# One more pause in the conversion of a MoE1 weight slot: two steps become three

## The chip, the cores and the metric

The kernel runs on one core of a Trainium2 chip. The core has a matrix engine (TensorE, PE in the profile), a vector engine (VectorE, DVE), an activation engine (ScalarE, ACT), a general engine (GpSimd, POOL) and a queue that issues most transfers (SyncE, SP). Each engine works through its own list of instructions in order; engines wait for each other through semaphores. The metric is the device time of one execution in microseconds (us); lower is better.

## The reference

```python
def reference(**kwargs):
    ...
    attn_out = _attn_ref(**attn_kwargs)          # q, k, v: 2 x 12 heads x 448 x 64, causal
    B, H, S, D = attn_out.shape
    x = np.ascontiguousarray(attn_out.transpose(0, 2, 1, 3)).reshape(B * S, H * D)   # 896 x 768
    x = _moe_ref(x=x, **moe_kwargs)              # h = x @ w_in (768 x 2048); h * sigmoid(1.702 h) @ w_out
    return _moe2_ref(x=x, **moe2_kwargs)         # 8 experts, one for each token: relu(x @ w1[e]) @ w2[e]
```

The two weights of the middle part, `w_in` (768 x 2048) and `w_out` (2048 x 768), reach the kernel as 64-bit floats.

## The kernel before

The program is written out by hand, engine by engine, in one order (`tc.manual_schedule()`): what stands earlier in the code stands earlier in each engine's list. It has four stages.

**Attention.** 12 pairs of heads, 7 query blocks a pair: 84 steps `s`, whose place in a pair is `s % 7`. A step puts scores on PE (`qk`, L374), their row maximum on DVE (`nmax`, L386), the exponential on ACT (`P`, L388), the normalisation on DVE (`rc`, L395 and L396) and POOL (`P`, L397), and four steps later the transposition of P on PE (`p_tr`, L405) and its copy out of PSUM (`pT`, L408 on DVE or L410 on ACT). Once a pair `av` (L423) sums the output, which ACT and DVE split into a high and a low part (`xhi`, L429, and `xlo`, L430).

**MoE1, first layer ("l1").** 16 blocks `f` of 128 columns of `w_in`, in four quarters `fq`, each of 6 parts `kk` of the inner dimension. For one `kk` PE does 6 matmuls (L444: high by high, high by low, low by high, each for two groups of tokens). Even blocks take their two PSUM tiles from a ring of three ("sc"), odd blocks from one of four ("tp"): the second tile of an even block is the first tile of the even block before it. After the matmuls of a block, ACT (`g`, L547) and DVE (`g`, L548) empty its PSUM in four pieces.

**MoE1, second layer ("l2").** First part B (256 columns) for 7 groups of tokens `t`, then part A (512 columns) for the same 7; 16 parts `kk` each, three matmuls a part (L587). Every four parts ACT and DVE split one more piece of the hidden layer (`gs`, L516 and L519), three pieces ahead. Small PE transpositions and logits (L627, L639) hang on ACT's copies (`y`, L609, and `yT`, L629).

**MoE2.** The experts' weights come as 32-bit floats into 24 places and are split by ACT and DVE (`split`, L307 and L308). The first of them are called for in part A as soon as the last slot of MoE1 is converted (`fill`).

**The weight slots of MoE1.** 48 pieces of `w_in` and `w_out` (24 for l1, 8 for part B, 16 for part A), 128 x 512, are converted from 64-bit floats into a high and a low part: DVE puts the bits together in `w` (L226, L228, L232), ACT rounds `w` into the high part (L234), DVE subtracts it for the low part (L235). One such conversion is a Python generator (`work`, in `add64`). `Stream.pump(n)` adds n to a credit and draws the generator on by one step for each whole credit, at places written into the other stages: at `s % 7` = 3 and 6 in attention, once for each `kk` in l1 (twice in the last quarter), and at the small rates `R2` and `R3` in l2. A step that starts a slot needs a free place in a ring of 19 (`RA`); if there is none, the step does nothing. When the generator ends, the slot is ready, its raw buffer (5, `RAW`) is given back and the next load is put on SP's list (`prefetch`). The subtraction is kept in `st.late` and put on DVE's list in the first step of the slot that follows. A slot that is needed and not ready is drawn to its end at once (`need`).

Of the kernel before, what the change touches and what calls it, by code (L numbers as in the profile page):

```python
# [115 lines left out]
def kernel(ctx, tc, q, k, v, w_in, w_out, w_gate, w_og, w1, w2, out):  # L116
# [49 lines left out]
    with tc.manual_schedule():  # L166
# [43 lines left out]
        def raw_tile(where, shape, dt):  # L210
            if where == "raw":
                return raws.tile(shape, dt, name="raw", tag="raw", bufs=RAW)
            return ringA.tile(shape, dt, name="rawA", tag=f"slotA{where}")

        def add64(keys, src, two=False, ring="A"):
            def load(where):
                raw = raw_tile(where, [128, 512], I64)
                nc.sync.dma_start(raw.rearrange("p (a n) -> p a n", a=2) if two else raw, src)
                return raw

            def work(keys, raw):
                slot = st.slots[keys[0]] = ring_slot(keys[0])
                r = raw.bitcast(U32).rearrange("p (n two) -> p n two", two=2)
                w = raws.tile([128, 512], F32, name="w32", tag="w32", bufs=2)
                wu = w.bitcast(U32)
                nc.vector.tensor_scalar(wu, r[:, :, 1], 3, 0x3FFFFFF8,  # L226
                                        op0=ALU.logical_shift_left, op1=ALU.bitwise_and)
                nc.vector.scalar_tensor_tensor(wu, r[:, :, 1], 0xC0000000, wu,  # L228
                                               op0=ALU.bitwise_and, op1=ALU.bitwise_or)
                st.flush()  # L230
                yield
                nc.vector.scalar_tensor_tensor(wu, r[:, :, 0], 29, wu,  # L232
                                               op0=ALU.logical_shift_right, op1=ALU.bitwise_or)
                nc.scalar.copy(slot[:, 0], w)  # L234
                st.late = keys[0], lambda: nc.vector.tensor_sub(slot[:, 1], w, slot[:, 0].bitcast(F32))  # L235

            st.add(keys, ring, load, work)
# [3 lines left out]
        def ring_slot(key):  # L241
            ring, place = st.home[key]
            if ring == "A":
                return ringA.tile([128, 2, 512], F32R, name="slotA", tag=f"slotA{place}")
            return xr_p[0].tile([128, 2, 512], F32R, name="slotX", tag=f"slotX{place}")
# [792 lines left out]
```

## Time and profile before

| | |
|---|---|
| median of 3 runs | 625.28 us (625.07 to 625.89) |
| the profiled execution's own time | 625.63 us |
| its span, first to last instruction | 623.5 us |
| PE busy | 590.3 us (95%) |
| DVE busy | 463.9 us (74%) |
| ACT busy | 376.9 us (60%) |
| mean granted TensorE clock | 0.987 |

The busy time of PE is modelled at the ends of its matmuls, so a busy PE can still be held up a little. Idle time of an engine counts only where the engine that sets the end waits too. A row of the timeline shows when an instruction started and how long it took, and in brackets how long its engine had been idle and whose result ended that.

### The profile page before, as it was taken

Reading aid. Unit: us, or ns where it says so; the run is one execution under the profiler, and the core shown is the slowest. Engines: PE = TensorE matmul, PEld = TensorE weight load, DVE = VectorE, ACT = ScalarE, POOL = GpSimd, SP = SyncE. Lnnn points to the kernel's source line nnn. Section 1 sums busy time; section 2 is a strip of 40 time slices with the busy share of each in tenths; the row PEclk is TensorE's granted clock in tenths of the full one; section 3 lists DMA queues with packets and bytes.
Section 4 is the critical chain, followed back from the end, with each engine's and each line's share of the span. In section 5 each row is a group of like instructions: output and inputs, shape, how many; then the busy total and the mean of one; then the engine's idle time right before and its main releaser. Section 6 shows DMA issues by size and latency. Waiting matters only on the chain. (4 is left out here: it accounts for less than half of the span.)

```text
span 623.5 us, 10060 instructions
## 1 busy us (share of the span) xinstructions
PE 590.3 (95%) x3326; PEld 473.6 (76%) x3326; DVE 463.9 (74%) x942; ACT 376.9 (60%) x743; POOL 106.7 (17%) x225
## 2 busy tenths in 40 slices
PE   7999999899979999889999999989999999999995
PEld 4665665578868888879877777767888888888884
DVE  2788888757858483797633447789998898889886
ACT  4878878623232323455433234678888888888885
POOL 3333333310000000000001002231631111001110
PEclk8999999999979999999999999999999999999998
DMA  5856554216434241433571503359999999999940
GB/s 134 245 125 141 123 126 116 56 57 184 142 111 115 89 136 37 143 116 119 176 263 38 150 17 119 111 183 347 349 368 353 318 383 377 380 381 378 383 161 20
DMA packets 93146, 118.02 MB, mean 189 GB/s; under 512 B 40208, under 2 KB 53408, under 8 KB 93090
## 3 DMA queue, kind: packets, MB, share of 16 engines
q1 hardware_dynamic: 88562, 109.05, 54.7%
q0 software_dynamic: 2512, 5.54, 2.5%
q10 hardware_dynamic: 2016, 2.75, 1.2%
q8 instruction: 28, 0.46, 0.4%
q14 instruction: 28, 0.23, 0.1%
HBM read 114.10 MB, written 7.54 MB: 195 GB/s over the span
## 5 line engine op out<-in xcount | busy, mean ns | idle before, releaser
L587 PE MATMUL py<-slotA,gs 128*128 128x256 f32 (+1 forms) x609 | 112.5, 337 | 1.0 <-DVE gs L519 1.0
L444 PE MATMUL ph<-xhi,slotA 128*128 128x512 f32 (+1 forms) x384 | 97.7, 374 | 5.6 <-DVE g L548 5.6
L587 PEld LDWEIGHTS py<-slotA,gs 128*128 128x128 f32 x609 | 90.8, 190 | 13.6 <-issue 2.6
L444 PEld LDWEIGHTS ph<-xhi,slotA 128*128 128x128 f32 x384 | 70.8, 191 | 16.5 <-issue 6.1
L234 ACT CAST slotA<-w 128x512 fp32r<-128x512 f32 x45 | 27.9, 621 | 63.1 <-DVE w L232 61.4
L308 DVE TENSOR_TENSOR ent<-wraw,ent 128x1024 fp32r<-128x1024 f32 x48 | 57.9, 1221 | 5.8 <-ACT ent L307 5.8
L444 PE MATMUL ph<-xlo,slotA 128*128 128x512 f32 x192 | 56.1, 373 | 0.0
L374 PE MATMUL sc<-kT,qz 128*128 128x64 f32 (+6 forms) x168 | 53.2, 401 | 2.8 <-ACT kT L365 2.4
L388 ACT ACTIVATE P<-sc,nmax 128x64 f32<-128x64 f32 (+6 forms) x84 | 40.3, 479 | 24.5 <-DVE nmax L386 14.7
L548 DVE TENSOR_TENSOR g<-ph,g 128x256 f32<-128x256 f32 x64 | 23.6, 389 | 41.5 <-ACT g L547 41.5
L897 PE MATMUL ps_h<-ent,xh 128*128 128x512 f32 x192 | 54.0, 402 | 0.0
L307 ACT CAST ent<-wraw 128x1024 fp32r<-128x1024 f32 x48 | 49.9, 1053 | 0.0
L519 DVE TENSOR_TENSOR gs<-g,gs 128x512 fp32r<-128x512 f32 x56 | 37.5, 683 | 16.6 <-ACT gs L516 16.6
L397 POOL TENSOR_SCALAR P<-P,rc 128x64 f32<-128x64 f32 (+2 forms) x72 | 36.0, 500 | 69.6 <-DVE rc L396 43.5
L516 ACT CAST gs<-g 128x512 fp32r<-128x512 f32 x56 | 33.8, 618 | 16.3 <-PE py L587 10.6
L386 DVE TENSOR_REDUCE nmax<-sc 128x1 f32<-128x64 f32 (+6 forms) x84 | 34.4, 411 | 10.7 <-PE sc L375 10.7
L547 ACT ACTIVATE g<-ph 128x256 f32<-128x256 f32 x64 | 20.9, 355 | 33.5 <-PE ph L444 17.2
L897 PEld LDWEIGHTS ps_h<-ent,xh 128*128 128x128 f32 x192 | 35.0, 188 | 7.6 <-DVE ent L308 0.3
L308 DVE TENSOR_TENSOR ent<-wrb,ent 128x1024 fp32r<-128x1024 f32 x30 | 36.3, 1223 | 4.7 <-ACT ent L307 4.2
L444 PEld LDWEIGHTS ph<-xlo,slotA 128*128 128x128 f32 x192 | 35.8, 192 | 4.6
L405 PE MATMUL ps_pT<-ident,P 128*128 128x128 f32 x192 | 37.8, 289 | 1.1
L228 DVE SCALAR_TENSOR_TENSOR w<-raw,w 128x512 uint32<-128x512 uint32 x46 | 35.0, 762 | 1.6
(189 smaller groups left out, 1175.5 us busy)
## 6 DMA issues: line engine op xcount, KB each, us to landing
wraw<-in_moe_w_dram SPq DMA_DIRECT2D x66, 512.0 KB
wrb<-in_moe_w_dram SPq DMA_DIRECT2D x48, 512.0 KB
wr<-in_moe_w_dram SPq DMA_DIRECT2D x30, 512.0 KB
raw<-in_moe_w_in_dram SPq DMA_DIRECT2D x24, 512.0 KB
raw<-in_moe_w_out_dram SPq DMA_DIRECT2D x22, 512.0 KB
qraw<-in_q_dram SPq DMA_DIRECT2D x24, 112.0 KB
kraw<-in_k_dram SPq DMA_DIRECT2D x24, 112.0 KB
vraw<-in_v_dram SPq DMA_DIRECT2D x24, 96.0 KB
```

Source lines behind the costliest of these rows:

```text
L228: nc.vector.scalar_tensor_tensor(wu, r[:, :, 1], 0xC0000000, wu, op0=ALU.bitwise_and, op1=ALU.bitwise_or)
L307: nc.scalar.copy(hi, raw)
L308: nc.vector.tensor_sub(lo, raw, hi.bitcast(F32))
L374: nc.tensor.matmul(sc[:, :n], qT[:, j].rearrange("d h p -> d (h p)"), kT[:, :n], start=True, stop=False)
L386: nc.vector.tensor_reduce(nm, sc[:, :n], axis=AX.X, op=ALU.max, negate=True)
L388: nc.scalar.activation(Pb[j][:, :n], sc[:, :n], AF.Exp, bias=nm, scale=1.0, accum_out=sm)
L397: eng[NORM_ENG[j]].tensor_scalar(Pb[j][:, :n], Pb[j][:, :n], rc, 1.0, op0=ALU.mult, op1=ALU.mult)
L405: nc.tensor.transpose(ps[:, c].rearrange("p h q -> p (h q)"), Pb[j][:, c * KC:(c + 1) * KC], ident)
L444: nc.tensor.matmul(p[:, 0:128 * nt], wt, xt[:, kk, 128 * t0:128 * (t0 + nt)], start=kk == 0 and n == 0, stop=kk == KD - 1 and n == 2)
L519: glate.append(lambda: nc.vector.tensor_sub(gs[:, 1], src, gs[:, 0].bitcast(F32)))
L587: nc.tensor.matmul(py[:, :n], gt[:, kk % 4], wt, start=kk == 0 and m == 0, stop=kk == KF - 1 and m == 2)
L897: nc.tensor.matmul(hps[hf], xh[:, k0 + n], wt[:, n], start=k0 + n == 0 and m == 0, stop=False)
```

## The change

A `yield` is put between ACT's rounding and the last statement of the generator.

```diff
                 nc.vector.scalar_tensor_tensor(wu, r[:, :, 0], 29, wu,
                                                op0=ALU.logical_shift_right, op1=ALU.bitwise_or)
                 nc.scalar.copy(slot[:, 0], w)
+                yield
                 st.late = keys[0], lambda: nc.vector.tensor_sub(slot[:, 1], w, slot[:, 0].bitcast(F32))
```

The number of pumps is not changed. The step that is added puts no instruction on DVE, ACT or PE; it ends the generator, which gives back the raw buffer and puts the next load on SP's list. So three draws convert a slot where two did. The order of instructions on PE and on POOL stays as it is. On DVE, ACT and SP the instructions of the slots move to later places among the others; none is added or taken away. Line numbers behind L234 grow by one in the changed kernel (L235 becomes L236, L386 becomes L387, L548 becomes L549).

By the pumps, 12 slots were begun in attention before (11 of them converted to the rounding there), and 8 are now. In l1 before, blocks 1 to 4 converted three slots each, block 5 one, block 6 none, blocks 7 and 8 three each, blocks 9 and 10 none, blocks 11 and 12 three each; now blocks 1 to 11 convert two each, block 12 four and block 13 three. At the end of l1 37 slots are ready in both. In part B 2.4 slots a group at the rate 0.3 become 1.6; the last two slots, of which only the end of the last stood in part A before, are now converted in the first four parts of part A, and `fill` is called four parts later there.

The places on DVE's list follow. In attention, the second pair that is pumped, around the place `s % 7` = 6: `xlo` of the pair before, the maximum of the largest block but one, and behind it the step of a slot. Before:

```order
L430 TENSOR_TENSOR xlo<-ps_o,xhi 128x448
L396 RECIPROCAL rc<-rc 128x1
L386 TENSOR_REDUCE nmax<-sc 128x1
L232 SCALAR_TENSOR_TENSOR w_533<-raw,w_533 128x512
L386 TENSOR_REDUCE nmax<-sc 128x1
```

The same place in the changed kernel:

```order
L431 TENSOR_TENSOR xlo<-ps_o,xhi 128x448
L397 RECIPROCAL rc<-rc 128x1
L387 TENSOR_REDUCE nmax<-sc 128x1
L226 TENSOR_SCALAR w_593<-raw 128x512
L228 SCALAR_TENSOR_TENSOR w_593<-raw,w_593 128x512
L236 TENSOR_TENSOR slotA<-w_382,slotA 128x512
L387 TENSOR_REDUCE nmax<-sc 128x1
```

The three instructions that begin a slot, which stood at `s % 7` = 3 in every pair, stand here in every third pair; that pair has none at `s % 7` = 3.

In l1, DVE's list of block 1 from the first slot up to where the block is emptied. Before, three slots:

```order
L226 TENSOR_SCALAR w_2038<-raw 128x512
L228 SCALAR_TENSOR_TENSOR w_2038<-raw,w_2038 128x512
L235 TENSOR_TENSOR slotA<-w_1979,slotA 128x512
L232 SCALAR_TENSOR_TENSOR w_2038<-raw,w_2038 128x512
L226 TENSOR_SCALAR w_2059<-raw 128x512
L228 SCALAR_TENSOR_TENSOR w_2059<-raw,w_2059 128x512
L235 TENSOR_TENSOR slotA<-w_2038,slotA 128x512
L232 SCALAR_TENSOR_TENSOR w_2059<-raw,w_2059 128x512
L226 TENSOR_SCALAR w_2080<-raw 128x512
L228 SCALAR_TENSOR_TENSOR w_2080<-raw,w_2080 128x512
L235 TENSOR_TENSOR slotA<-w_2059,slotA 128x512
L232 SCALAR_TENSOR_TENSOR w_2080<-raw,w_2080 128x512
```

In the changed kernel, two, and then the four instructions that empty block 1:

```order
L226 TENSOR_SCALAR w_2002<-raw 128x512
L228 SCALAR_TENSOR_TENSOR w_2002<-raw,w_2002 128x512
L236 TENSOR_TENSOR slotA<-w_1900,slotA 128x512
L232 SCALAR_TENSOR_TENSOR w_2002<-raw,w_2002 128x512
L226 TENSOR_SCALAR w_2029<-raw 128x512
L228 SCALAR_TENSOR_TENSOR w_2029<-raw,w_2029 128x512
L236 TENSOR_TENSOR slotA<-w_2002,slotA 128x512
L232 SCALAR_TENSOR_TENSOR w_2029<-raw,w_2029 128x512
L549 TENSOR_TENSOR g_1973<-ph_1993,g_1973 128x2x128
L549 TENSOR_TENSOR g_1974<-ph_1993,g_1974 128x2x128
L549 TENSOR_TENSOR g_1975<-ph_1994,g_1975 128x2x128
L549 TENSOR_TENSOR g_1976<-ph_1994,g_1976 128x128
```

A slot's four instructions stand one after the other in both; four of them have left the block.

## Rows read from the trace of the kernel before

**Rows 1.** Busy time by stage: stretch, its length, each engine, granted clock, DMA share.

```profile
121.00:252.00 131.00, 124.67 (x600) 107.94 (x599) 84.48 (x174) 39.41 (x95) 4.83 (x46) 0.97 0.38 110
252.00:310.00 58.00, 53.35 (x410) 48.87 (x409) 47.83 (x89) 30.42 (x61) 0.74 (x1) 1.00 0.41 129
```

**Rows 2.** The same for a full attention pair, then the first pumped pair.

```profile
39.34:48.81 9.47, 8.96 (x64) 5.67 (x62) 8.23 (x28) 7.59 (x25) 3.42 (x8) 1.00 0.56 129
...
21.06:29.87 8.81, 8.72 (x63) 5.67 (x62) 7.09 (x26) 7.33 (x24) 3.19 (x7) 1.00 0.74 251
```

**Rows 3.** Timeline of DVE, attention: start, duration, what, idle before it.

```profile
40.80 0.41 DVE L226 TENSOR_SCALAR w<-raw 128x512 uint32<-128x512 uint32 x1
41.24 1.01 DVE L228 SCALAR_TENSOR_TENSOR w<-raw,w 128x512 uint32<-128x512 uint32 x1
...
42.77 0.28 DVE L386 TENSOR_REDUCE nmax<-sc 128x1 f32<-128x128 f32 x1
...
45.46 0.54 DVE L386 TENSOR_REDUCE nmax<-sc 128x1 f32<-128x384 f32 x1
45.91 0.76 DVE L232 SCALAR_TENSOR_TENSOR w<-raw,w 128x512 uint32<-128x512 uint32 x1
46.59 0.21 DVE L386 TENSOR_REDUCE nmax<-sc 128x1 f32<-128x64 f32 x1
```

**Rows 4.** Timeline of POOL and PE in the same pair.

```profile
41.05 0.66 POOL L397 TENSOR_SCALAR P<-P,rc 128x448 f32<-128x448 f32 x1 [0.53 <-DVE rc L396]
...
47.31 0.59 POOL L397 TENSOR_SCALAR P<-P,rc 128x384 f32<-128x384 f32 x1 [1.18 <-ACT slotA L234]
...
47.96 0.55 PE L405 MATMUL ps_pT<-ident,P 128*128 128x128 f32 x3
...
49.80 0.97 PE L423 MATMUL ps_o<-pT,vraw 128*64 128x448 f32 x4 [0.41 <-DVE pT L408]
```

**Rows 5.** Timeline of DVE in l1.

```profile
136.30 0.42 DVE L226 TENSOR_SCALAR w<-raw 128x512 uint32<-128x512 uint32 x1
...
166.46 0.42 DVE L226 TENSOR_SCALAR w<-raw 128x512 uint32<-128x512 uint32 x1
...
168.73 0.42 DVE L226 TENSOR_SCALAR w<-raw 128x512 uint32<-128x512 uint32 x1
...
174.32 0.42 DVE L548 TENSOR_TENSOR g<-ph,g 128x256 f32<-128x256 f32 x1 [0.97 <-ACT g L547]
...
176.50 0.42 DVE L226 TENSOR_SCALAR w<-raw 128x512 uint32<-128x512 uint32 x1
```

**Rows 6.** Timeline of PE in l1.

```profile
155.63 0.41 PE L444 MATMUL ph<-xhi,slotA 128*128 128x384 f32 x1 [0.61 <-DVE g L548]
...
168.69 0.99 PE L444 MATMUL ph<-xhi,slotA 128*128 128x512 f32 x4
...
169.93 0.81 PE L444 MATMUL ph<-xhi,slotA 128*128 128x512 f32 x3
175.76 0.66 PE L444 MATMUL ph<-xhi,slotA 128*128 128x384 f32 x1 [5.02 <-DVE g L548]
...
251.81 0.34 PE L444 MATMUL ph<-xhi,slotA 128*128 128x384 f32 x1
```

**Rows 7.** Short stretches in l1, columns as in Rows 1.

```profile
174.00:174.50 0.50, 0.00 (x0) 0.00 (x0) 0.18 (x1) 0.28 (x1) 0.00 (x0) 0.89 0.56 184
...
181.00:181.50 0.50, 0.50 (x3) 0.40 (x3) 0.44 (x2) 0.02 (x1) 0.00 (x0) 0.78 1.06 414
```

**Rows 8.** Timeline of PE in part B of l2.

```profile
257.67 3.62 PE L587 MATMUL py<-slotA,gs 128*128 128x256 f32 x28 [0.97 <-DVE gs L519]
...
277.68 0.44 PE L627 MATMUL ps_yT<-ident,y 128*128 128x128 f32 x2 [1.81 <-ACT y L609]
...
287.69 3.86 PE L587 MATMUL py<-slotA,gs 128*128 128x256 f32 x30
...
294.19 3.86 PE L587 MATMUL py<-slotA,gs 128*128 128x256 f32 x30
```

## Prediction

> **What bounds the kernel now.** I read the page first: PE is busy for 95% of the span, so only the remaining waits can be won or lost by an edit that adds no work. Busy time by stage puts a good part of them where slots are converted: PE is not busy for 6.3 us of l1 (131.0 less 124.67) and for 4.65 us of part B [rows 1]. In attention a pair takes 9.47 us, of which DVE is busy for 8.23, while the first pair that is pumped, which carries no subtraction yet, took 8.81 [rows 2]. So DVE, not PE, sets the pace wherever slots crowd on it. The timelines say how.
>
> In attention, the instructions at the head of a slot take from 40.80 to 42.77, 1.97 us, and the third instruction of the slot takes 0.68 (45.91 to 46.59) [rows 3]. All maxima queue behind them; the chain goes on over ACT, DVE and POOL, and PE waits at its end: the 128x384 normalisation on POOL starts at 47.31, ends at 47.90, and the transposition that needs it starts at 47.96; then PE waits 0.41 for DVE's copy of that transposition [rows 4].
>
> In l1 a slot takes 2.27 us of DVE (166.46 to 168.73), three of them 7.86 up to the first piece of the emptying (174.32), and from there to the next block's first slot 2.18 (176.50) [rows 5]. That is 10.04 for a block. PE needs 1.24 for a `kk` (168.69 to 169.93), 7.44 for a block [rows 6]. With three slots a block, DVE falls 2.6 us back each time until PE has no PSUM to write to: 0.61 at 155.63 and 5.02 at 175.76 [rows 6]. During the second wait the granted clock fell from full (2.4 GHz) to half: it averages 0.89 over 174.0 to 174.5, so it fell near 174.39, and 0.78 over 181.0 to 181.5, so it was back near 181.2 [rows 7]. PE had last worked at 170.74 (169.93 plus 0.81), 3.65 us ahead of the fall. From 175.76 to 181.2 it did half of what it could: 2.7 us lost on top of the wait.
>
> **What the change does.** It adds no instruction; it spreads the same ones. There are four terms.
>
> **Attention, about 2.2 us gained.** The pumps now run through a cycle of three pairs. The first pair is as before (9.47). The second has its 1.97 at the later place and nothing at the earlier one. The third has only the 0.68. The third pair loses DVE's 1.97 and has nothing at the later place; leaving the pair's own waits aside, PE's list of a pair comes to about 8.4: the 8.81 of the first pumped pair [rows 2] less some 0.4 that PE's starts show as gaps in it, which is an estimate. So it gains about 1.0. The second pair is the disputed one. Where 0.68 stood, the head of a slot and a subtraction now stand ahead of the small block's maximum (46.59) [rows 3]. They take 1.66 to 1.97: 2.27 less the 0.61 that its last instruction takes in l1 by the gap between neighbours (an estimate), or as in rows 3. I take 1.75, 1.07 more. The maximum of the 128x384 block, at 45.46, can come some 0.36 sooner, because nothing stood at the earlier place; so 0.7 later remains. That goes straight into POOL's start at 47.31 and PE's at 47.96 [rows 4]. Of this PE would have waited 0.41 a moment later anyway, and DVE's later copy is only about 0.3 late, since ACT has no rounding to do ahead of the small block's exponential. I take 0.2 lost a pair. Ten pairs follow the first: three as before, four of the second kind, three of the third: 3.0 less 0.8. Bounds: if the second kind is as good as the first pumped pair (8.81), four times 0.65 more is gained, 5.6 in all; if it pays all of 1.07 plus 0.1 for an unlucky overlap, 1.7 is lost.
>
> GpSimd may make the later place dearer or cheaper. DVE's second instruction took 1.01 at 41.24 [rows 3] while POOL's 41.05 to 41.71 ran [rows 4]; the whole slot in l1, with POOL idle, takes 2.27, against 1.97 plus 0.68 here. The Trainium skill, "GPSIMD Engine Reference", Specifications, says that GpSimd shares its SBUF interfaces with VectorE and that they contend when a VectorE instruction has two SBUF inputs, as this one has. By the rows alone the head costs 1.75; by that rule, with POOL's work beside it each time, 1.97, and the attention term would be 1.4 instead of 2.2. The trace agrees with the rule in that one overlap and does not show the later place.
>
> **l1, about 1.0 us gained.** Two slots a block make DVE's block 10.04 less 2.27, 7.77 us, against PE's 7.44: 0.33 a block behind instead of 2.6. That is what PSUM run-ahead can hold up to block 11. Then come four slots and three slots, because the last quarter pumps twice for each `kk`. DVE's clock: block 1's first slot at 136.30; its emptying starts 5.59 later (7.86 less 2.27), 141.89; block 11's ten times 7.77 later, 219.59; block 12's first slot at 221.77, its emptying four slots later (10.13) at 231.90. PE resumed 1.44 after such a start (174.32 to 175.76), so block 14's second tile is free at 233.34. PE would want it eight blocks after 170.74, less the 0.6 to 0.8 of the wait at 155.63 that no longer occurs: 229.5. It waits about 3.9 us: one wait for block 12's PSUM instead of block 4's. DVE sets this end, so it hardly depends on PE. From 233.34 PE has 71 matmuls of 1.24/6 left, 14.7 us: 248.0, where before the last started at 251.81 [rows 6] and ended some 0.2 later. That would be a gain of 4.0. But 3.9 is beyond the 3.65 after which the clock fell in the only wait as long. If it falls again, another 2.7 to 3.2 us are lost. I take that: 1.0 gained. Bounds: 4.0 with a full clock; and, if each block costs DVE 0.05 more (10.09, the next pair of neighbouring blocks), 0.3.
>
> **Part B, about 3.3 us gained.** A group with 2.4 slots costs DVE 5.4 for slots, four subtractions of about 0.6 (an estimate from neighbouring starts) and 0.2 for logits: 8.0. PE needs 6.50 (287.69 to 294.19) [rows 8]. So DVE lags, ACT's rounding waits for DVE, ACT's copies for PE wait behind it, and PE waits up to 1.81 for one. With 1.6 slots DVE needs 6.2, below PE. Of the 4.65 idle [rows 1], the 0.97 at 257.67 [rows 8] stands behind a slot head that does not move; the other 3.7 should nearly go. I keep 0.4 of it for groups 5 and 6, which had no slots and now have. Bounds: 0 and 3.7.
>
> **Part A, the loads and MoE2, nothing.** Two slots, 4.5 us of DVE, move into part A's first four `kk`. The pieces of the hidden layer are made three ahead, 12 `kk`, and hide it; without that cover it would cost the 4.5. On SP the raw loads come later but five slots ahead still; the q, k and v loads behind them in attention are called for two pairs ahead. The eleven loads of `fill` come four `kk` later, their users only at the last group of part A. If the cover were gone, that is up to 3 us.
>
> **Sum.** 2.2 + 1.0 + 3.3 = 6.5. The profiled execution took 625.63 (span 623.5 and 2.1 around it), 0.35 above the median; 625.3 less 6.5 is 618.8 us.
>
> **Rivals.** (a) The clock stays full in block 14's wait. For it: 3.9 and 3.65 are within what DVE's pace leaves open. l1 then gives 3.7 rather than 1.0: 616.1. (b) The pairs of the second kind are as quick as the first pumped pair, because DVE's list is 0.68 shorter: 3.4 more gained in attention: 615.4. Against it: POOL's chain at 47.31 has no slack. (c) Slower: the later place is worse than the earlier one. DVE reaches it with PE already waiting on POOL. If each such pair pays the whole 1.97, and its delay runs into the third pair, which then gains nothing, attention loses 7.9 and the rest gives 4.3: 628.9. It decides from 5.6 us lost in attention on; the third kind's two missing slots speak against it. (d) The yield moves work but attention and l1 stay paced as now, the gain of one wait becoming the next: only part B's 3.3 or half of it is left, or the later `fill` takes it back: 624.5, no change by 0.2%.
>
> **How the numbers follow.** Forecast 0.42 (617 to 621), (a) 0.26, (b) 0.14, (c) 0.08, (d) 0.10. The range takes in (a) and (b) with their own play and leaves (c) and most of (d) out: 613.5 to 623. A measurement of this kernel tells about 0.2%, 1.25 us, from no change. Faster 0.83, same 0.09, slower 0.08.
>
> **What would show it.** In the profile after: pairs of 9.5, 9.7 and 8.4 us in turn; no wait of PE for `g` before block 12, and one of 3 to 5 us at block 14, with the clock at half behind it; in part B one wait near 1 us and no 1.8; part A and MoE2 of the same length. I am wrong if the pairs do not alternate, if PE waits for `g` at an earlier block too, or if DVE is still behind in part B.

## The result, and the profile after

Four runs of the changed kernel took 619.58 us in the median (619.01 to 619.98), four of the kernel before, on the same chip, 625.58: a ratio of 0.9904, 95% interval 0.9887 to 0.9921. The profiled execution took 619.69 us, its span 617.6, against 625.63 and 623.5. First, the page of the kernel after, busy time by engine:

```profile
span 617.6 us, 10059 instructions
## 1 busy us (share of the span) xinstructions
PE 588.5 (95%) x3326; PEld 473.5 (77%) x3326; DVE 461.8 (75%) x942; ACT 377.6 (61%) x743; POOL 106.1 (17%) x225
```

The work is the same; what changed is waiting. Where it changed is read from four landmarks on PE, each the start of a row of the timeline: the multiplication of P with v of attention's last pair ("last `ps_o`"), the first `py` of part B, the first row of part A behind the transposition of part B's last `y` (some 1.5 us into part A, in both kernels), and the first matmul of MoE2 (`ps_x`).

| from, to | before, us | after, us | gained |
|---|---|---|---|
| start, last `ps_o` of attention | 124.89 | 124.57 | 0.32 |
| to the first `py` (l1) | 127.10 | 125.03 | 2.07 |
| part B | 51.76 | 48.01 | 3.75 |
| part A | 84.92 | 84.89 | 0.03 |
| MoE2, to the end of the span | 234.9 | 235.1 | -0.2 |

Windows of the kernel after, the two stretches of [rows 1] and then three pairs of attention in a row, as [rows 2]; columns are the length, busy time of PE, weight loads, DVE, ACT and POOL, granted clock, DMA share and GB/s:

```profile
121.00:252.00 131.00, 125.56 (x616) 108.95 (x615) 93.15 (x190) 42.78 (x103) 4.36 (x46) 0.99 0.40 122
252.00:310.00 58.00, 56.77 (x420) 51.54 (x419) 47.84 (x88) 29.94 (x60) 0.00 (x0) 1.00 0.48 152
...
31.48:41.04 9.56, 8.68 (x62) 5.64 (x62) 7.36 (x27) 7.33 (x25) 3.40 (x9) 1.00 0.47 124
41.04:49.94 8.90, 8.81 (x63) 5.67 (x62) 6.30 (x25) 7.64 (x26) 3.66 (x9) 1.00 0.39 99
49.94:59.39 9.45, 8.95 (x62) 5.66 (x61) 8.20 (x28) 7.58 (x26) 3.39 (x9) 1.00 0.59 127
```

In attention the pairs alternate: 9.56, 8.90, 9.45 (the prediction's second, third and first kind), where all were 9.47. The timeline of the kernel after shows what the 9.56 is made of (DVE, POOL, PE; start, duration, idle before it and its releaser):

```profile
36.74 0.42 DVE L226 TENSOR_SCALAR w<-raw 128x512 uint32<-128x512 uint32 x1
37.19 0.69 DVE L228 SCALAR_TENSOR_TENSOR w<-raw,w 128x512 uint32<-128x512 uint32 x1
37.80 0.68 DVE L236 TENSOR_TENSOR slotA<-w,slotA 128x512 fp32r<-128x512 f32 x1
38.40 0.22 DVE L387 TENSOR_REDUCE nmax<-sc 128x1 f32<-128x64 f32 x1
...
39.05 0.99 POOL L398 TENSOR_SCALAR P<-P,rc 128x384 f32<-128x384 f32 x2 [2.18 <-DVE rc L397]
...
39.68 0.55 PE L406 MATMUL ps_pT<-ident,P 128*128 128x128 f32 x3 [0.88 <-POOL P L398]
...
228.30 0.81 PE L445 MATMUL ph<-xhi,slotA 128*128 128x512 f32 x3
233.57 0.43 PE L445 MATMUL ph<-xhi,slotA 128*128 128x384 f32 x1 [4.46 <-DVE g L549]
...
255.29 3.62 PE L588 MATMUL py<-slotA,gs 128*128 128x256 f32 x28 [0.99 <-DVE gs L520]
...
272.18 0.44 PE L628 MATMUL ps_yT<-ident,y 128*128 128x128 f32 x2 [0.24 <-ACT y L610]
```

At the later place of the pair the head of the slot and the subtraction take 1.66 us (36.74 to 38.40), where a single instruction took 0.68 [rows 3]. L228 takes 0.69 there, not the 1.01 it took beside POOL, for POOL is idle from 36.87 to 39.05. In both traces it is the same each time: 1.01 in the 13 cases in which it meets POOL's 128x448 normalisation (ten before, three now), 0.69 to 0.70 in all others. The small block's maximum is late by what is left of it, POOL's normalisation with it, and PE waits 0.88 for POOL instead of 0.41 for DVE [rows 4].

In l1 the two waits of before, 0.61 and 5.02 [rows 6], are gone, and one of 4.46 has come at block 14. The clock fell in it again. The windows of the kernel after around the wait:

```profile
233.00:234.00 1.00, 0.43 (x2) 0.46 (x3) 0.76 (x2) 0.45 (x2) 0.00 (x0) 0.92 0.77 279
234.00:237.00 3.00, 3.00 (x10) 2.62 (x9) 2.86 (x6) 0.32 (x2) 0.00 (x0) 0.50 0.13 53
237.00:237.50 0.50, 0.50 (x3) 0.40 (x3) 0.47 (x1) 0.36 (x1) 0.00 (x0) 0.76 0.00 0
```

A mean of 0.92 puts the fall at 233.84, 0.27 us after PE had resumed, one of 0.76 the return at 237.24. PE worked at half speed in between and lost half of these 3.40 us, 1.7; before it was 175.76 to 181.2, 2.7 us lost [rows 7]. In part B one wait near 1 us is left and one of 0.24; the 1.81 of before [rows 8] is gone.

### The profile page after: what moved, and what is told of

It is laid out like the page before. It is cut to its first block, busy times and chain, and to the rows that moved or that the text cites. A ratio compares the mean times of both kernels' runs of the same rounds, so it can differ in the third digit from the quotient of the medians.

```text
span 617.6 us, 10059 instructions
## 1 busy us (share of the span) xinstructions
PE 588.5 (95%) x3326; PEld 473.5 (77%) x3326; DVE 461.8 (75%) x942; ACT 377.6 (61%) x743; POOL 106.1 (17%) x225
## 5 line engine op out<-in xcount | busy, mean ns | idle before, releaser
L234 ACT CAST slotA<-w 128x512 fp32r<-128x512 f32 x45 | 27.9, 620 | 76.9 <-DVE w L232 76.8
L387 DVE TENSOR_REDUCE nmax<-sc 128x1 f32<-128x64 f32 (+6 forms) x84 | 34.5, 415 | 17.7 <-PE sc L376 17.6
L549 DVE TENSOR_TENSOR g<-ph,g 128x256 f32<-128x256 f32 x64 | 23.7, 390 | 30.9 <-ACT g L548 30.5
L406 PEld LDWEIGHTS ps_pT<-ident,P 128*128 128x128 f32 x192 | 21.2, 141 | 20.9 <-POOL P L398 17.2
L228 DVE SCALAR_TENSOR_TENSOR w<-raw,w 128x512 uint32<-128x512 uint32 x46 | 32.8, 713 | 1.6
```

Of the source, the lines that this page charges most:

```text
L387: nc.vector.tensor_reduce(nm, sc[:, :n], axis=AX.X, op=ALU.max, negate=True)
L406: nc.tensor.transpose(ps[:, c].rearrange("p h q -> p (h q)"), Pb[j][:, c * KC:(c + 1) * KC], ident)
```

## The experiments

Each kernel was timed beside the kernel before; ratios are to those runs. Counted in DVE's list from one block's emptying in l1 to the next, the kernel before draws 12 slots up to the emptying of block 0, then 3, 3, 3, 3, 1, 0, 3, 3, 0, 0, 3, 3 and none; the changed one 8, then eleven times 2, then 4, 3 and none.

**Is it the step, or the rate?** The third step puts nothing on DVE, ACT or PE: in it the generator only ends, the slot becomes usable and its raw buffer free. So it may matter only in that a slot takes three pumps. First, three steps and one and a half times the pumps:

```diff
-    R1, R1B = 1, 2
-    R2 = (0.1, 0.3, 0.3, 0.3, 0.15, 0.3, 0.2)
-    R3 = (1.2, 1.2, 1.2, 1.2, 1.2, 1.2, 1.2)
+    R1, R1B = 1.5, 3
+    R2 = (0.15, 0.45, 0.45, 0.45, 0.225, 0.45, 0.3)
+    R3 = (1.8, 1.8, 1.8, 1.8, 1.8, 1.8, 1.8)
...
-                st.pump(1)
+                st.pump(1.5)
```

> The third step stays, but every pump is made half as large again, so that a slot is converted as often as before the change. My theory (the gain is the thinner spread of DVE's work, the step itself costs and gives nothing): as before the change, 625.5 us, within 1 us, with the 5 us wait of PE in l1 and the 1.8 us wait in part B back. Rival (the later end of a slot, with its later load and later subtraction, gives the gain): 619.6 us, as with the change.

It took 627.64 us (626.84 to 628.67), ratio 1.0027 [1.0014, 1.0040]: all the gain is gone, and 1.8 us more than that (625.87 before). Waits of PE in the timeline of this kernel:

```profile
155.71 0.41 PE L445 MATMUL ph<-xhi,slotA 128*128 128x384 f32 x1 [0.61 <-DVE g L549]
175.84 0.66 PE L445 MATMUL ph<-xhi,slotA 128*128 128x384 f32 x1 [5.03 <-DVE g L549]
257.61 3.61 PE L588 MATMUL py<-slotA,gs 128*128 128x256 f32 x28 [0.97 <-DVE gs L520]
278.83 0.61 PE L628 MATMUL ps_yT<-ident,y 128*128 128x128 f32 x2 [2.32 <-ACT y L610]
```

In l1 they are the waits of [rows 6] to within 0.01 us, and the pairs are 9.46 again. Part B is 2.9 longer than before (54.62 against 51.76): the rate is the same, but other pumps draw the steps there. The long wait for `y` is 2.32 instead of 1.81 [rows 8], and the clock is at half behind it, from 278.96 to 282.37, which costs half of these 3.4 us.

**The counter-trial:** two steps, as before, and pumps of two thirds.

```diff
-    R1, R1B = 1, 2
-    R2 = (0.1, 0.3, 0.3, 0.3, 0.15, 0.3, 0.2)
-    R3 = (1.2, 1.2, 1.2, 1.2, 1.2, 1.2, 1.2)
+    R1, R1B = 0.6667, 1.3334
+    R2 = (0.0667, 0.2, 0.2, 0.2, 0.1, 0.2, 0.1334)
+    R3 = (0.8, 0.8, 0.8, 0.8, 0.8, 0.8, 0.8)
...
-                st.pump(1)
+                st.pump(0.6667)
```

> The kernel before with its two steps and no third, but every pump counted for two thirds of what it was (0.6667 in attention and l1, 1.3334 in l1's last quarter, 0.2 for 0.3 in part B, 0.8 for 1.2 in part A). Theory (the third step does no work on any engine, so it acts as a rate of two thirds and as nothing else): the same slots in every block of l1, the same three kinds of pair in attention, one wait of about 4.5 us at block 14, part B about 48.0 us, the whole 619.6 us (618.5 to 620.5) like the changed kernel. Rival (the step matters by itself, as by raw buffers given back one pump later): over 1.3 us away from 619.6.

It took 626.38 us (624.73 to 627.14), ratio 1.0009 [0.9996, 1.0022]: the theory, taken at its number, failed. But the profiled execution (625.08 us) shows a single place. l1 took 125.02 us and part B 48.04, as in the changed kernel; the first pumped pair took 14.15 us instead of 9.36, 4.8 of the 5.4 us between the two profiled executions. Timeline of this kernel, SP, DVE and PE:

```profile
25.98 0.92 SPq L348 DMA_DIRECT2D vraw<-in_v_dram  x2
...
27.59 2.86 SPq L218 DMA_DIRECT2D raw<-in_moe_w_in_dram  x5
...
32.10 0.43 DVE L226 TENSOR_SCALAR w<-raw 128x512 uint32<-128x512 uint32 x1 [4.30 <-DMA raw<-in_moe_w_in_dram]
...
34.45 0.55 PE L405 MATMUL ps_pT<-ident,P 128*128 128x128 f32 x3 [4.67 <-POOL P L397]
```

The same loads and the first slot in the changed kernel:

```profile
17.70 2.64 SPq L218 DMA_DIRECT2D raw<-in_moe_w_in_dram  x4
25.64 0.91 SPq L349 DMA_DIRECT2D vraw<-in_v_dram  x2
...
23.39 0.43 DVE L226 TENSOR_SCALAR w<-raw 128x512 uint32<-128x512 uint32 x1 [0.72 <-DMA raw<-in_moe_w_in_dram]
```

The first pump that draws a step also issues the first raw loads. At 0.6667 that is the second pump; by then the pair's loads of v stand ahead in SP's list and go out only at 25.98, and the raw loads came 9.9 us later. DVE stood 4.30 us for them with the pair's maxima queued behind. If that is all, the count needs only a start value:

```diff
-        self.credit = 0.0
+        self.credit = 0.6667
```

> As the kernel with two steps and pumps of two thirds, but the count begins at 0.6667 instead of 0, so that the first pump already draws a step, as in the changed kernel. Theory (rate alone; what the other kernel lost, it lost once, at its first slot, whose loads are called by the first pump that draws: there they came 10 us later, behind loads of v that wait for buffers, and PE waited 4.67 us): no wait at the first pumped pair, pairs of 9.56, 8.90 and 9.45 us, l1 125.0 us, part B 48.0 us, the whole 619.6 us (618.5 to 620.5). Rival (the step matters by itself, or the slower start was not the cause): 623 us or more.

It took 619.87 us (618.62 to 620.13), ratio 0.9895 [0.9878, 0.9911]: the changed kernel's time without a third step, with pairs of 9.56, 8.90 and 9.45 us, a wait of 4.44 at block 14 and a part B of 48.02. Only l1 is not as expected: 126.0, since the clock was at half there from before PE's return (233.08) to 238.34. So the change is a rate of two thirds, and its phase matters at the first slot.

**One stage at a time.** The yield is taken only where a flag says so; the flag is switched at the end of attention and at the end of l1.

```diff
-                yield
+                if st.three:
+                    yield
```

> Three steps only in attention. My theory: attention gives about 0.9 us, but l1 then has 29 slots to convert at three a block; DVE is 2.3 us longer behind for each of the four, PE meets a second wait of some 5 us at block 10 with the clock at half behind it, about 8 us: 632.5 us, 628 to 634. Rival (a slot moved from attention to l1 costs nothing there, because PE's wait is bounded by the ring of places): 624.6 us.

Attention alone took 633.43 us (632.36 to 634.89), ratio 1.0121 [1.0099, 1.0143]: it makes the kernel slower, by about what was forecast. The waits of PE in l1 in this kernel:

```profile
155.96 0.41 PE L447 MATMUL ph<-xhi,slotA 128*128 128x384 f32 x1 [1.00 <-DVE g L552]
176.04 0.66 PE L447 MATMUL ph<-xhi,slotA 128*128 128x384 f32 x1 [4.97 <-DVE g L552]
214.04 0.66 PE L447 MATMUL ph<-xhi,slotA 128*128 128x384 f32 x1 [5.09 <-DVE g L552]
```

Attention still ended at 124.83. But four slots fewer are ready when l1 begins (8 instead of 12), they fall into blocks that already draw three, and a third wait comes at block 10, with the clock at half once more (212.70 to 219.52): l1 took 135.7 us instead of 127.1.

> Three steps only in l1; attention and part B with two. My theory: attention hands over 12 slots, so l1 spreads 25 instead of 29, two a block, and block 12's four come when DVE has caught up in block 10; PE meets no wait of more than 1 us and l1 gives back all of its 8.3 us: 617.3 us, 616 to 619. Rival (what counts is the number of slots and not their spread, or the last blocks' crowd costs a wait here too): l1 gives the 2.1 us that it gave with the whole change: 623.4 us.

l1 alone took 620.28 us (618.88 to 621.60), ratio 0.9919 [0.9901, 0.9937]: between the two forecasts. In the profiled execution, 618.88, l1 gained 6.2 us: one wait of 1.86 at block 14 is left, with the clock full behind it.

> Three steps only in l2. My theory: part B gives the same 3.7 us as with the whole change, since it begins with 37 slots in any case, and nothing else moves: 621.8 us, 621 to 622.6. Rival (part B gained because DVE arrived there less late from l1): no change, 625.5 us.

l2 alone took 622.03 us (621.85 to 622.64), ratio 0.9942 [0.9925, 0.9959], as expected; part B took 48.00, l1 kept its waits. Alone, the stages give -7.6, 5.6 and 3.8, together 1.9; the whole change gave 6.0. They do not add, because with two slots a block l1 takes attention's four slots without a new wait before block 14.

> Three steps in l1 and l2, two in attention. Theory (the stages add up): the 5.3 us that l1 alone gained and the 3.8 us that part B alone gained, 625.6 - 9.1 = 616.5 us (615 to 618); attention pairs 9.46 us, block 14 of l1 waits 1.9 us, part B 48.0 us. Rival (part B's gain in the changed kernel came from slots that attention left undone or did for it): part B stays near 51.7 and the whole is 620.3 us.

l1 and l2, without attention, took 617.18 us (616.28 to 617.97), ratio 0.9859 [0.9835, 0.9882], 2.4 below the whole change; 8.7 us are gained, of the 9.4 that the two alone make. Its timeline and windows at the wait in block 14:

```profile
228.69 0.81 PE L447 MATMUL ph<-xhi,slotA 128*128 128x512 f32 x3
231.36 0.48 PE L447 MATMUL ph<-xhi,slotA 128*128 128x384 f32 x1 [1.86 <-DVE g L552]
...
231.00:232.00 1.00, 0.64 (x2) 0.64 (x3) 0.66 (x3) 0.45 (x3) 0.00 (x0) 0.78 0.00 0
```

The same place with l1 alone:

```profile
228.07 0.81 PE L447 MATMUL ph<-xhi,slotA 128*128 128x512 f32 x3
230.74 0.41 PE L447 MATMUL ph<-xhi,slotA 128*128 128x384 f32 x1 [1.86 <-DVE g L552]
...
231.00:232.00 1.00, 1.00 (x6) 0.91 (x6) 0.70 (x2) 0.51 (x2) 0.00 (x0) 1.00 0.00 0
```

The wait is the same, 1.86 us; the clock fell to half in one and stayed full in the other. It does not account for the 2.7 us over which the runs with l1 alone spread: the slowest of them, 621.60, has a mean granted clock of 0.994, the fastest, 618.88, one of 0.993. What makes that spread stays open.

**What sets a pair of attention?** The change with no slot drawn in attention at all:

```diff
-    PUMP_FROM, PUMP_PAST, L1_PAST = 7, 9, 1
+    PUMP_FROM, PUMP_PAST, L1_PAST = 999, 9, 1
```

> The change with no slot drawn in attention at all (all of them later, before and in l1, which gets longer), so only the pace of the attention pairs is to be read. Theory (a pair without slot work is bound by PE's list, some 8.4 us): pairs of 8.3 to 8.5 us. Rival (the chain over ACT, DVE and POOL, or PE's own waits, hold a pair at 8.8 to 8.9 us without any slot): pairs of 8.8 to 8.9. The whole time says nothing here; l1 is expected to be some 10 us longer.

One run, 630.58 us. Windows of one pair:

```profile
31.27:39.93 8.66, 8.66 (x63) 5.64 (x62) 5.81 (x24) 7.23 (x25) 3.42 (x9) 1.00 0.36 80
```

The floor is 8.66 us, and PE is busy for all of it: neither my 8.4 nor the rival's 8.8 to 8.9. The third kind, at 8.90, pays 0.24 for its 0.68 of DVE and its rounding on ACT. Is it the rounding? The yield moved ahead of it:

```diff
-                nc.scalar.copy(slot[:, 0], w)
                 yield
+                nc.scalar.copy(slot[:, 0], w)
```

> The change with the yield ahead of ACT's rounding instead of behind it, so the rounding goes to the third step together with the subtraction. Theory (ACT's rounding, which now stands ahead of the 128x128 exponential at the early place of the third kind of pair, holds that pair at 8.90 us): the third kind falls to about 8.5, the second kind, where head and rounding had met, also loses its rounding, the first takes it on: a cycle of three of 27.5 us instead of 27.9 and a whole of 618.5 us (617 to 619.6) if l1 is as in the change. Rival (PE's own floor of a pair is 8.9): the third kind stays at 8.85 to 8.95 and the whole at 619.6 us, or above it where the subtraction now waits for ACT.

It took 619.00 us (618.10 to 619.32), ratio 0.9886 [0.9863, 0.9908], within what a measurement can tell of the change's. Starts of the multiplication with v, one for each pair:

```profile
40.71 0.97 PE L424 MATMUL ps_o<-pT,vraw 128*64 128x448 f32 x4
...
49.80 0.97 PE L424 MATMUL ps_o<-pT,vraw 128*64 128x448 f32 x4 [0.36 <-DVE pT L409]
...
58.78 0.97 PE L424 MATMUL ps_o<-pT,vraw 128*64 128x448 f32 x4
...
68.67 0.60 PE L424 MATMUL ps_o<-pT,vraw 128*64 128x448 f32 x2
```

The pairs are 9.09, 8.98 and 9.89 (third, first, second kind), 27.96 in all against 27.91: nothing is won in the cycle. The first kind, rid of a rounding, is 0.47 quicker, the second, with one at its early place, 0.33 slower; the expectation had these two the wrong way round. The third, whose rounding went from the early to the later place, is 0.19 slower. That does not clear the rounding at the early place, as ACT's timeline shows: when the output's high part comes (`xhi`) in a third pair of the changed kernel (from 41.04), in a pair without slots (from 39.93) and in the third pair here (from 40.71), and the rounding here.

```profile
44.90 0.55 ACT L430 CAST xhi<-ps_o 128x448 fp32r<-128x448 f32 x1
...
43.45 0.53 ACT L430 CAST xhi<-ps_o 128x448 fp32r<-128x448 f32 x1 [0.19 <-PE ps_o L424]
...
44.24 0.53 ACT L430 CAST xhi<-ps_o 128x448 fp32r<-128x448 f32 x1 [0.19 <-PE ps_o L424]
46.72 0.61 ACT L235 CAST slotA<-w 128x512 fp32r<-128x512 f32 x1
```

That is 3.86 us into the pair with the rounding at the early place, 3.52 and 3.53 without it. The maximum of the 128x384 block, which stands behind `xlo` on DVE, follows 0.27 late (5.05 against 4.78 in the pair without slots), POOL's normalisation of it 0.25 (6.91 against 6.66), and these are the 0.24 of the pair. So the theory had the cause right. The forecast failed because at the later place the rounding stands ahead of the small block's exponential and costs more, 0.43 over the 8.66.

**Where l1's wait comes from.** The whole change with single pumps in l1's last quarter, so no block draws more than two slots:

```diff
-    R1, R1B = 1, 2
+    R1, R1B = 1, 1
```

> The change, with one pump for each kk in l1's last quarter as in the others, so blocks 12 to 14 draw two slots each instead of four and three, and one slot fewer falls into l1. Theory (the four slots of block 12 are what makes block 14 wait): DVE stays 0.33 a block behind to the end, PE's 4.46 us of wait at block 14 and the 1.6 us that the half clock cost behind it are gone: l1 125.0 - 6.1 = about 119 us, and the whole is 613.5 us (613 to 615), with every other stage as in the change. Rival (DVE's slow lag over eleven blocks is enough, the last quarter only shows it): a wait of 3 us or more stays at block 14 or 15, and the whole is 618 to 620 us.

It took 616.21 us (616.08 to 617.30), ratio 0.9849 [0.9826, 0.9872]. The wait at block 14 is gone: from the last `ps_o` to the start of the last row of l1's matmuls it is 118.53 us instead of 124.62, the 6.1 that were expected. The whole lies between the two forecasts, though. The timeline of PE and the windows at the start of part B show a new wait and a new fall of the clock:

```profile
242.07 0.57 PE L445 MATMUL ph<-xhi,slotA 128*128 128x512 f32 x2
244.68 0.50 PE L588 MATMUL py<-slotA,gs 128*128 128x256 f32 x2 [2.04 <-ACT gs L517]
...
246.00:247.00 1.00, 1.00 (x9) 1.00 (x8) 1.00 (x2) 1.00 (x3) 0.00 (x0) 0.71 0.00 0
```

With slots drawn up to block 14, DVE empties that block late; ACT's first pieces `gs` of the hidden layer stand behind it, and PE waits for them. The clock fell to half in the matmuls that follow, and part B took 50.33 instead of 48.01: 2.0 and 2.3 of the 6.1 went back. (Of the 3.4 us between the two profiled executions 1.0 lies at the start and 0.7 in MoE2.) The cure is to have no slots in the last blocks:

> Three steps in l1 and l2 alone, and one pump for each kk of l1's last quarter, so no block of l1 draws more than two slots and blocks 14 and 15 draw none. Theory (all that is left to win in l1 is the one wait of 1.86 us at block 14 and the stretch of half clock that may follow it; the slots end two blocks ahead of part B, so part B starts without waiting): no wait of PE for g, l1 from 122.4 to about 119.2 us, part B 48.0 us, and the whole at 617.2 - 3.0 = about 614.2 us (613.5 to 615.5). Rival (as with the single pumps in the full change, what l1 gains is given back at part B's start, in a wait for the first pieces of the hidden layer): a wait of some 2 us at the start of part B, a part B of 50 us, and 616 us or more.

Three steps in l1 and l2 alone and single pumps (both diffs above) took 614.63 us (614.28 to 615.54), ratio 0.9824 [0.9811, 0.9838], as forecast. Windows of its l1:

```profile
124.58:243.60 119.02, 119.02 (x581) 103.50 (x582) 81.84 (x166) 37.53 (x90) 2.58 (x22) 1.00 0.39 118
```

PE is busy for all of l1, at a full clock. Part B is longer, 48.96, with waits of 1.24, 0.39 and 0.39 for ACT's copies `y`. Last, the same rate with two steps (pumps of 1 in attention, 0.6667 in all of l1, two thirds in l2):

> Two steps as before, pumps as before in attention, two thirds in all of l1 (its last quarter too, 0.6667) and in l2: the schedule of the fastest kernel so far, without a third step. Theory (rate alone): 614.6 us (613.6 to 615.6), no wait of PE for g in l1. Rival (the step by itself gave part of it): 616 us or more.

It took 612.70 us (612.56 to 612.89), ratio 0.9789 [0.9773, 0.9805], the fastest of all and below what was forecast. Windows of its l1 and part B:

```profile
125.28:244.30 119.02, 119.02 (x581) 103.57 (x582) 81.69 (x166) 38.42 (x90) 2.57 (x22) 1.00 0.39 117
...
244.30:291.28 46.98, 46.80 (x381) 44.10 (x381) 41.86 (x78) 27.04 (x55) 0.74 (x1) 1.00 0.34 107
```

l1 is the same; part B is 1.98 shorter, the 2.02 of waits. By the pump counts, two steps at 0.2 for each `kk` come every 5 `kk`, three at 0.3 put the two that work 3.3 apart and then leave 6.7. That would explain it, but was not tried apart, and it cannot be all: with two steps and the same rates the kernel with the right phase took 48.02 for part B, with three steps l2 alone took 48.00. Where the count stands when part B begins matters too.

## Why the prediction was right, and which terms were off

The forecast was 618.8 (617 to 621 for the likeliest case, 613.5 to 623 in all); 619.58 came. By the profiled executions 5.94 us were gained where the sum said 6.5. The sum is nearer than its terms: attention gave 1.9 less than forecast, l1 and part B 1.5 more. That these nearly cancel is luck.

**Attention, 2.2 forecast, 0.87 found** from the first to the last `ps_o`, 0.32 with a start that was 0.55 later. The mis-sized term was the third kind of pair: 8.4 was the first pumped pair less some 0.4 of gaps before PE's starts, but PE was busy for 8.72 of that pair's 8.81 [rows 2], the floor without any slot is 8.66, and ACT's rounding, which the term left out, makes it 8.90. It gave 0.57 each, not 1.0. The second kind was dear as argued, though less so: 9.56 against 9.67, with a head of 1.66 against 1.75; the dearer price of 1.97 needed POOL at work beside it, which was idle. And the last pair, the fourth of the second kind, where only one pair's work is left, took 9.31 instead of 8.81; I had not priced it apart. What the term leaves out is larger: attention hands l1 four slots more, and without them (l1 and l2 alone) the kernel is 2.4 faster by the medians.

**l1, 1.0 forecast, 2.07 found.** The waits were right in each step: two slots a block (DVE's blocks 7.78 us apart against 7.77), no wait before block 12, and one at block 14. The clock fell too, but the reason given for it, that 3.9 is more than 3.65, does not hold: over the runs it fell between 1.89 and 5.13 us after PE's last work (last section). The wait was 4.46 rather than 3.9: PE came 0.4 sooner (229.11) and was released 0.23 later (233.57). The clock was mis-sized: I took 2.7 to 3.2 for it from the fall in [rows 7], and it cost 1.7. That is not a property of the schedule: in the two-thirds kernel with the right phase, which has the same slots in every block, the half clock lasted 5.26 us behind PE's return and cost 2.6. That the last quarter's double pumps made the wait was shown by their removal.

**Part B, 3.3 forecast, 3.75 found;** l2 alone gave the same 3.8 with the other stages untouched. The 0.97 that was to stay stayed (0.99), and groups 5 and 6 cost nothing visible.

**Part A, the loads and MoE2, 0 forecast,** 0.03 gained and 0.2 lost. The loads were covered here, but the two-thirds kernel shows how near the limit lay: 4.7 us when the first ones came a pump later.

**The rivals.** (a) The clock fell, so its 616.1 did not come (with the 4.0 that the l1 term gives for a full clock it would have been 615.8). (b) The second kind took 9.56, not 8.81. (c) The later place did not cost 1.97, and its delay did not eat the third pair's gain. A slower kernel was indeed within reach, but by another way than (c): the slots that attention leaves over, if l1 keeps three a block. (d) Attention and l1 did not stay paced as before; in l1, though, one wait did take the place of another.

## What to carry to other kernels

An extra empty step in a queue of work is a change of rate, so read it stage by stage: what DVE needs for a block (here 7.77 us with two slots, 10.04 with three) against what PE needs (7.44), and count the slots that each block really draws, with those that an earlier stage leaves over. Then set the rate for each stage by itself, spread the steps evenly, and leave the blocks before a stage's end free: that gave 612.7 us where the change gave 619.6. When a rate is changed, look at the first item too, since its loads may be issued by the first step that is drawn.

## What the runs showed of the hardware

The length of PE's wait decided neither whether the clock fell nor when. It fell 4.73 us after PE's last work in the changed kernel (229.11 to 233.84) and 3.65 after it before [rows 7]. In the two-thirds kernel with the right phase, with the same wait at the same place, it fell 2.88 after (228.64 to 231.52); the timeline and windows of that kernel:

```profile
233.08 0.66 PE L444 MATMUL ph<-xhi,slotA 128*128 128x384 f32 x1 [4.44 <-DVE g L548]
...
231.00:232.00 1.00, 0.00 (x0) 0.00 (x0) 0.37 (x1) 0.60 (x2) 0.00 (x0) 0.76 0.53 201
...
238.00:239.00 1.00, 1.00 (x6) 0.90 (x6) 0.97 (x3) 0.48 (x1) 0.00 (x0) 0.83 0.91 373
```

Two more kernels have the same slots in l1 and that wait, the first one with two thirds (4.44) and the one with the rounding in the third step (4.47). There it fell 5.13 and 1.89 after. What it cost in these four kernels goes by how long it stayed at half behind PE's return: 3.40, 5.26, 3.41 and 4.24 us. Half of that taken off l1's 125.03, 126.01, 125.02 and 125.43 leaves 123.3 to 123.4 in all four.

With l1 and l2 alone the clock fell 2.06 after (229.50 to 231.56), and in the same wait of 1.86 with l1 alone, in a program that is the same up to there, not at all. With single pumps it fell at 246.42, 1.7 us after PE had begun to work again. The Trainium skill, "TensorE: Matmul & The Clock Gate", Part 1, says that the hardware watches activity in windows that run on their own, so that the same kernel can differ from run to run; the two waits of 1.86 and the four of 4.4 to 4.5 agree with that, but no run here shows the windows themselves.

The start differs as well. The program is the same up to the third pair's transposition of q, which began between 20.70 us (single pumps) and 22.11 (no slots in attention) in the profiled executions. In the changed kernel PE's clock was 0.66 on average from 14 to 16 us, and 1.00 before the change, and that transposition began 0.55 later. A difference below 1.4 us between two single executions can be this start alone.
